# Group outputs scaled behind the next dense part, V copies on two engines, x of chunk 1 behind two Q stores

## The chip, the cores and the metric

The kernel runs on one core of one Trainium2 chip. The metric is the device time of one execution in microseconds; medians of several executions are given, with the lowest and highest beside them. TensorE is called PE, VectorE DVE, ScalarE ACT and GpSimd POOL, as in the profile. The span of a profile is about 2 us shorter than the time of the same execution. "Granted clock" is the share of full speed that the throttle granted TensorE; it is 0.998 to 1.000 unless told otherwise.

## The reference

A transformer block with both branches on the same normalised input, 2048 tokens of 640 features, in bf16:

```python
xn = layernorm(x)                                   # no weights
q, k, v = split(xn @ wqkv)                          # 32 heads of 20
s = q @ k.T * 20 ** -0.5                            # masked: 0 <= i - j < 256
A = (softmax(s) @ v) @ wo
B = (sigmoid(xn @ w_gate) * (xn @ w_up)) @ w_down   # 1536 wide
out = x + A + B
```

## The kernel before

The tokens are worked off in four chunks of 512. Attention runs as a chain of steps (scores, exponentials, masks, product with V), and between two steps a "fill" puts dense matmuls: gate and up, Q, K, V of the next chunk, the down product with Wo. So PE's order is fixed in the program, and PE waits where another engine or a transfer is late. Three PSUM banks (the buffers that PE writes products into; at 51 us PE is listed as waiting 0.34 us for h to free one) turn among all dense products; there is one score buffer, one accumulator `acc`, one `th` tile and five staging tiles `st`.

The loads at the start, all on one issuing queue:

```python
load_gu(0)                   # first half of gate and up weights
load_x(1)                    # x of chunk 1
clear("q", 0); clear("k", 0) # zero the padding of the Q and K scratch
...                          # Q and K of chunk 0, then load_rest()
```

Q and K pass through scratch in device memory; Q is copied by DVE, K by ACT, and both use the `st` tiles, so that the first K copy waits for the first Q store (6.37 us listed in the profile before):

```python
def proj_block(w, c, m):
    ps = ps_d.tile([P, CW], FP32, name="pqk", tag="d")
    ...                                    # 5 matmuls
    st = stp.tile([P, CW], BF16, name="st")
    if w == "q":
        nc.vector.tensor_copy(out=st, in_=ps)
    else:
        nc.scalar.copy(out=st, in_=ps)
    nc.sync.dma_start(out=dst[:, 4 * m:4 * m + 4, :], in_=st)
```

The normalisation of the next chunk runs beside gate and up; POOL computes the reciprocal root:

```python
def rstd_block(mv):
    rstd = lnp.tile([P, 1], FP32, name="rstd")
    nc.gpsimd.tensor_scalar(out=rstd, in0=mv[:, 1:2], scalar1=EPS, scalar2=None, op0=ADD)
    nc.gpsimd.tensor_tensor(out=rstd, in0=rstd, in1=neghalf, op=POW)
    return rstd
```

Gate and up: `th` by ACT from one bank, `h` by DVE from the next. And the end of a head group: DVE transposes the accumulator, then scales it:

```python
def finish_group(c, g, acc):
    t1 = np_.tile([P, 16, 32], FP32, name="t1")
    nc.vector.transpose(out=t1..., in_=acc)
    rec = np_.tile([P, 16, 1], FP32, name="rec")
    nc.vector.reciprocal(rec, t1[:, :, DH:VW])
    for m, slot, first, n in pieces_of(g):
        ...
        nc.vector.tensor_tensor(out=on[m]..., in0=t1..., in1=rec..., op=MULT)
        if slot + n == 32:
            nc.vector.transpose(out=oc[c, m], in_=on[m]...)
```

The fill's order, with the three parts that bring the output weights (`wo_i` is a rearranged copy of Wo in device memory, made by four transfers; `wo` loads it):

```python
fill.add("gu0", ...); fill.add("x2", ...)
fill.add("wd", later(load_wd), 0)
fill.add("qk1", g_qk(1), 50 * MM); fill.add("v1", g_v(1), 40 * 136)
fill.add("wo_i", later(turn_wo), 0)
fill.add("gu1a", ...)
fill.add("wo", later(load_wo), 0)
fill.add("out0", ...)
...
```

The softmax here doesn't subtract the row's maximum and nothing guards it: scores larger than these inputs give would overflow.

Of the kernel before, what the change touches and what calls it, by code (L numbers as in the profile page):

```python
# [18 lines left out]
NCH = S // CW  # L19
SBC = CW // P  # L20
HG = 4
NG = H // HG
# [78 lines left out]
def pieces_of(g):  # L101

    f, left, src = g * DH, DH, 0
    while left:
        m, p = divmod(f, 32)
        n = min(left, 32 - p)
        yield m, p, src, n
        f, left, src = f + n, left - n, src + n
# [3 lines left out]
def kernel(  # L112
# [11 lines left out]
    nc = tc.nc  # L124
# [31 lines left out]
    def load_x(c):  # L156
        t = xp.tile([P, SBC, D], BF16, name="xc")
        xc[c] = t
        nc.sync.dma_start(out=t, in_=xr[:, c * SBC:(c + 1) * SBC, :])
# [33 lines left out]
    def clear(w, k):  # L193
        rows = scratch[w, k].rearrange("(h j) s -> h (j s)", j=32)[:, DH * CW:]
        nc.sync.dma_start(out=rows.rearrange("h (a e) -> h a e", a=4), in_=zero[:, 0:3, :])

    def load_gu(k):
        for t, w in ((wg, B_w_gate), (wu, B_w_up)):
            nc.sync.dma_start(out=t[k], in_=w.rearrange("(c p) f -> p c f", p=P)[:, :, k * FS:(k + 1) * FS])

    load_gu(0)
    load_x(1)
    clear("q", 0)
    clear("k", 0)

# [84 lines left out]
    def proj_block(w, c, m):  # L290


        base = 0 if w == "q" else D
        ps = ps_d.tile([P, CW], FP32, name="pqk", tag="d")
        for d in range(DC):
            wt = wqkv[:, d, base:base + D].rearrange("p (k m) -> p m k", m=DC)
            nc.tensor.matmul(ps, lhsT=wt[:, m, :], rhs=xnT[c][:, d, :],  # L297
                             start=(d == 0), stop=(d == DC - 1))
# [5 lines that stand above are left out]
        dst = scratch[w, c % 2].rearrange("(h j) s -> h j s", j=32)  # L304
        nc.sync.dma_start(out=dst[:, 4 * m:4 * m + 4, :], in_=st)

    def spread(w, c, g0, g1):

        if g0 == 0:
            qk[w, c] = (qp if w == "q" else kp).tile([P, NG, CW], BF16, name=w + "T")  # L310
        src = scratch[w, c % 2].rearrange("(g p) s -> p g s", p=P)
        nc.sync.dma_start(out=qk[w, c][:, g0:g1, :], in_=src[:, g0:g1, :])

    def new_v(c, s):
        v = vp.tile([P, H * VW + 11], BF16, name="v")
        vt[c * SBC + s] = v
        nc.gpsimd.memset(v[:, 0:H * VW].rearrange("p (h d) -> p h d", d=VW)[:, :, DH:VW], 0.5)
        nc.gpsimd.memset(v[:, H * VW:], 0.0)

    def project_v(c, s, hf):  # L320
        ps = ps_d.tile([P, CW], FP32, name="pv", tag="d")
        for d in range(DC):
            nc.tensor.matmul(ps[:, 0:HALF], lhsT=xnT[c][:, d, s * P:(s + 1) * P],  # L323
                             rhs=wqkv[:, d, 2 * D + hf * HALF:2 * D + (hf + 1) * HALF],
                             start=(d == 0), stop=(d == DC - 1))
        return ps

    def copy_v(c, s, hf, ps, copy):
        v3 = vt[c * SBC + s][:, 0:H * VW].rearrange("p (h d) -> p h d", d=VW)
        copy(out=v3[:, hf * 16:(hf + 1) * 16, 0:DH],  # L330
             in_=ps[:, 0:HALF].rearrange("p (h d) -> p h d", d=DH))

    def proj_v(c, s, hf, copy=nc.vector.tensor_copy):
        copy_v(c, s, hf, project_v(c, s, hf), copy)
# [26 lines left out]
    def g_qk(c):  # L361
        for w in "qk":
            for m in range(DC):
                proj_block(w, c, m)
                if w == "k" and m == 1:
                    spread("q", c, 0, NG if c else 2)
                yield 5 * MM
        if c == 0:
            spread("k", c, 0, 1)
            spread("k", c, 1, 3)  # L370
            spread("q", c, 2, 4)
            spread("k", c, 3, 4)

    def g_v(c):
        for s in range(SBC):
            new_v(c, s)
            for hf in range(2):
                proj_v(c, s, hf)
            if s == 0:
                spread("k", c, 0, 2)  # L380
                spread("k", c, 2, NG)
            yield 10 * 136
# [106 lines left out]
    def pv(c, g, parts):  # L489
        acc = ps_a.tile([P, CW], FP32, name="acc")  # L490
        flat = [(pt, *piece[1:]) for step, pt in parts for piece in step["pv"] if piece[0] == g]
        for k, (pt, r, q, n, col) in enumerate(flat):
            v = vt[c * SBC + r]
            for i in range(HG):
                h = g * HG + i
                nc.tensor.matmul(  # L496
                    acc[32 * i:32 * i + 32, q * U:(q + n) * U],
                    lhsT=v[:, h * VW:h * VW + 32], rhs=pt[:, i, col * U:(col + n) * U],
                    start=(k == 0), stop=(k == len(flat) - 1), skip_group_check=True)
        finish_group(c, g, acc)  # L500
# [3 lines left out]
    def finish_group(c, g, acc):  # L504
        t1 = np_.tile([P, 16, 32], FP32, name="t1")
        nc.vector.transpose(out=t1.rearrange("p b r -> p (b r)"), in_=acc)  # L506
        rec = np_.tile([P, 16, 1], FP32, name="rec")
        nc.vector.reciprocal(rec, t1[:, :, DH:VW])
        for m, slot, first, n in pieces_of(g):
            if slot == 0:  # L510
                on[m] = onp.tile([P, 16, 32], BF16, name="on")
            nc.vector.tensor_tensor(out=on[m][:, :, slot:slot + n], in0=t1[:, :, first:first + n],  # L512
                                    in1=rec.to_broadcast([P, 16, n]), op=MULT)
            if slot + n == 32:
                oc[c, m] = op.tile([P, CW], BF16, name="oc")
                nc.vector.transpose(out=oc[c, m], in_=on[m].rearrange("p b r -> p (b r)"))


    class Fill:
        def __init__(self):  # L520
            self.parts = []
            self.done = set()
            self.shut = set()

# [8 lines left out]
        def one(self):  # L533
            label, gen, _ = self.parts[0]
            try:
                cost = next(gen)
                self.parts[0][2] -= cost
                return cost
            except StopIteration:
                self.parts.pop(0)  # L540
                self.done.add(label)
                return 0

        def pull(self, ns):
            while ns > 0 and self.parts and self.parts[0][0] not in self.shut:
                ns -= self.one()
            return ns
# [72 lines left out]
    for _ in g_qk(0):  # L620
        pass
    load_rest()

    fill = Fill()
# [8 lines left out]
    fill.add("x2", later(load_x, 2), 0)  # L633
    fill.add("wd", later(load_wd), 0)
    fill.add("qk1", g_qk(1), 50 * MM)
    fill.add("v1", g_v(1), 40 * 136)
    fill.add("wo_i", later(turn_wo), 0)
    fill.add("gu1a", mix(g_gu(1, 0, 2), norms2, 0, 2, False), 2 * GU)
    fill.add("wo", later(load_wo), 0)
    fill.add("out0", mix(g_out(0), norms2, 0, 2), OUT)  # L640
    fill.add("x3", later(load_x, 3), 0)
    fill.add("qk2", g_qk(2), 50 * MM)
    fill.add("v2", g_v(2), 40 * 136)
    fill.add("gu1b", mix(g_gu(1, 2, 12), g_norms(3, False), 10), 10 * GU)
    fill.add("out1", mix(g_out(1), g_turns(3), 1, 3), OUT)
    fill.add("qk3", g_qk(3), 50 * MM)
    fill.add("v3", g_v(3), 40 * 136)
    fill.add("gu2", g_gu(2, 0, 12), 12 * GU)
    fill.add("out2", g_out(2), OUT)
# [14 lines left out]
    for t, (c, k, step) in enumerate(todo):  # L664
        if k == 0 and c > 0:
            fill.until(f"qk{c}")
        if k == 2 and c > 0:
            fill.until(f"v{c}")
        for group in [x for x in ends if ends[x] == t - 2]:
            pv(*group, parts.pop(group))  # L670
            if group[1] == NG - 1:
                fill.shut.discard(f"out{group[0]}")
        made = (step, scores(c, step))
        for g in dict.fromkeys(piece[0] for piece in step["pv"]):
            parts.setdefault((c, g), []).append(made)
        last, label = next(x for x in cuts if t < x[0])
        credit += fill.left(label) * step["units"] / sum(x[2]["units"] for x in todo[t:last])
        credit = fill.pull(credit)
    fill.pull(10 ** 9)

    c = NCH - 1

# [44 lines left out]
```

## Time and profile before

| | before |
|---|---|
| time, median of 3 runs | 319.24 us (319.14 to 319.47) |
| span of the profile | 317.7 us |
| PE idle in the span | 7.9 us, of which 3.2 are the listed idle time of the five stalls below |

PE is 97% busy, so the table that matters is that of its stalls (listed idle time plus overlap in the list). A stall is told here as the listed idle time plus the time by which matmuls that do not wait overlap in the list. The prediction takes 0.16 us for it. The lines themselves stand in the prediction.

| at us | PE waits for | stall |
|---|---|---|
| 22.4 | a bank that a K copy (ACT) frees, which waits for a Q store | 0.51 |
| 51.1 | a bank that h (DVE) frees | 0.50 |
| 89.1 | Wo | 1.58 |
| 199.5 | a bank that a V copy (DVE) frees | 0.67 |
| 272.3 | the score buffer, behind th and h | 0.66 |

### The profile page before, as it was taken

To read this page: it belongs to the slowest core of one execution; us is meant where nothing else is said; L and a number is where in the kernel's file an instruction comes from. 1 tells how busy PE (TensorE), PEld (TensorE's weight loads), DVE (VectorE), ACT (ScalarE), POOL (GpSimd) and SP (SyncE) were. 2 spreads that over 40 slices of the span, in tenths; PEclk is the share of its full clock that TensorE was granted. 3 is DMA by queue.
4 is the path that set the end of the run, shared out by engine and by line. 5 is a ranking of instruction groups with operands and counts; after the bars stand their busy time and mean duration, and the time that the engine had idled before them with its cause. 6 is when DMAs were issued, how large, how long until landed. Compare 5 with 4: busy or idle time off the path is not lost.

```text
span 317.7 us, 10276 instructions
## 1 busy us (share of the span) xinstructions
PE 309.8 (97%) x4393; PEld 174.6 (55%) x4393; DVE 160.1 (50%) x324; ACT 192.9 (61%) x243; POOL 177.8 (56%) x417
## 2 busy tenths in 40 slices
PE   7999999999989999999999999999999999999996
PEld 3654444456556655544566655544456664444674
DVE  4531486746854564556753553544552544363224
ACT  5713786786845458577654557576765667778200
POOL 3000487667768557575966637476466767576300
PEclk9999999999999999999999999999999999999999
DMA  7976967927744255500045035500000010000002
GB/s 250 371 284 185 321 212 116 314 86 223 233 107 48 64 172 177 182 11 3 0 53 77 23 105 165 186 1 3 2 2 23 26 43 3 2 2 2 0 2 83
DMA packets 34428, 33.05 MB, mean 104 GB/s; under 512 B 9648, under 2 KB 33840, under 8 KB 34352
## 3 DMA queue, kind: packets, MB, share of 16 engines
q1 hardware_dynamic: 34096, 32.17, 34.2%
q8 instruction: 34, 0.56, 0.7%
q10 hardware_dynamic: 288, 0.25, 0.3%
q14 instruction: 10, 0.08, 0.1%
HBM read 21.00 MB, written 10.26 MB: 98 GB/s over the span
## 4 chain that ended last, share of the span: by engine, by line
PE 80%; DMA 7%; ACT 4%; DVE 4%; POOL 2%; issue 1%; SPq 1%; ACTq 0%; POOLq 0%
PE pg L395 14%; PE y L415 14%; PE pu L402 14%; PE pqk L297 10%; PE ps L465 7%; PE acc L496 6%; PE y L428 6%; PE pv L323 5%; DMA wo_i<-in_A_wo_dram 2%; ACT pT L471 2%; DMA sq<-st 2%; PE d L415 2%; DMA sk<-st 1%; POOL pT L475 1%; DMA wo<-wo_i 1%
## 5 line engine op out<-in xcount | busy, mean ns | idle before, releaser
L475 POOL TENSOR_SCALAR_AFFINE_SELECT pT<-pT 128x256 bf16<-128x256 bf16 (+1 forms) x352 | 163.0, 497 | 117.9 <-ACT pT L471 117.8
L471 ACT ACTIVATE pT<-ps 128x1280 bf16<-128x1280 f32 (+2 forms) x152 | 147.4, 1023 | 70.4 <-PE ps L465 64.0
L406 DVE SCALAR_TENSOR_TENSOR h<-th,pu 128x512 bf16<-128x512 f32 x48 | 32.8, 684 | 57.8 <-PE pu L402 32.3
L395 PE MATMUL pg<-xnT,wg 128*128 128x512 bf16 x240 | 59.8, 380 | 0.3 <-DVE h L406 0.3
L402 PE MATMUL pu<-xnT,wu 128*128 128x512 bf16 x240 | 59.8, 380 | 0.0
L415 PE MATMUL y<-wd,h 128*128 128x320 bf16 x336 | 49.4, 300 | 0.0
L297 PE MATMUL pqk<-xnT,wqkv 128*128 128x512 bf16 x200 | 46.2, 381 | 0.4 <-ACT st L303 0.4
L415 PEld LDWEIGHTS <-h 128*128 128x128 bf16 x384 | 36.1, 98 | 14.4 <-issue 0.2
L506 DVE STREAM_TRANSPOSE t<-acc 128x512 f32<-128x512 f32 x32 | 22.8, 712 | 33.3 <-PE acc L496 32.9
L398 ACT ACTIVATE th<-pg 128x512 f32<-128x512 f32 x48 | 28.9, 602 | 17.3 <-DVE h L406 10.0
L402 PEld LDWEIGHTS <-wu 128*128 128x128 bf16 x240 | 22.0, 98 | 25.4 <-issue 0.6
L395 PEld LDWEIGHTS <-wg 128*128 128x128 bf16 x240 | 22.0, 98 | 25.2 <-issue 0.8
L465 PE MATMUL ps<-qT,kT 20*64 20x64 bf16 (+3 forms) x2048 | 32.8, 232 | 0.6 <-ACT pT L471 0.6
L465 PEld LDWEIGHTS <-kT 20*64 20x64 bf16 x2048 | 22.2, 104 | 20.2 <-issue 16.8
L297 PEld LDWEIGHTS <-wqkv 128*128 128x128 bf16 x200 | 22.5, 119 | 18.4 <-issue 1.2
L433 DVE SCALAR_TENSOR_TENSOR xn<-y,xc 128x320 bf16<-128x320 f32 x28 | 13.5, 490 | 30.8 <-PE y L428 30.8
L496 PE MATMUL acc<-pT,v 128*32 128x128 bf16 (+2 forms) x928 | 25.7, 250 | 0.0
L496 PEld LDWEIGHTS <-v 128*32 128x32 bf16 x928 | 16.9, 97 | 15.3 <-issue 11.0
L323 PE MATMUL pv<-wqkv,xnT 128*128 128x320 bf16 x160 | 24.0, 300 | 0.5 <-DVE v L330 0.5
L428 PE MATMUL y<-wo,oc 128*128 128x320 bf16 x140 | 21.2, 299 | 1.4 <-DMA wo<-wo_i 1.4
L512 DVE TENSOR_TENSOR on<-t,rec 128x320 bf16<-128x320 f32 (+4 forms) x48 | 20.5, 428 | 1.1
L428 PEld LDWEIGHTS <-oc 128*128 128x128 bf16 x160 | 15.3, 98 | 7.7 <-issue 1.7
(49 smaller groups left out, 151.3 us busy)
## 6 DMA issues: line engine op xcount, KB each, us to landing
qT<-sq SPq DMA_DIRECT2D x3, 1024.0 KB, 5.9
sq<-st SPq DMA_DIRECT2D x20, 128.0 KB, 2.4
sk<-st SPq DMA_DIRECT2D x20, 128.0 KB, 3.2
out_dram<-xn SPq DMA_DIRECT2D x15, 160.0 KB, 1.8
kT<-sk SPq DMA_DIRECT2D x3, 768.0 KB, 5.6
wg<-in_B_w_gate_dram SPq DMA_DIRECT2D x2, 960.0 KB, 7.6
wu<-in_B_w_up_dram SPq DMA_DIRECT2D x2, 960.0 KB, 12.0
xc<-in_A_x_dram SPq DMA_DIRECT2D x3, 640.0 KB, 12.0
```

Source lines behind the costliest of these rows:

```text
L297: nc.tensor.matmul(ps, lhsT=wt[:, m, :], rhs=xnT[c][:, d, :], start=(d == 0), stop=(d == DC - 1))
L323: nc.tensor.matmul(ps[:, 0:HALF], lhsT=xnT[c][:, d, s * P:(s + 1) * P], rhs=wqkv[:, d, 2 * D + hf * HALF:2 * D + (hf + 1) * HALF], start=( ...
L395: nc.tensor.matmul(pg, lhsT=part(wg, d, f), rhs=xnT[c][:, d, :], start=(d == 0), stop=(d == DC - 1))
L398: nc.scalar.activation(out=th, in_=pg, func=TANH, scale=0.5)
L402: nc.tensor.matmul(pu, lhsT=part(wu, d, f), rhs=xnT[c][:, d, :], start=(d == 0), stop=(d == DC - 1))
L406: nc.vector.scalar_tensor_tensor(out=h, in0=th, scalar=1.0, in1=pu, op0=ADD, op1=MULT)
L415: nc.tensor.matmul(ys[hf], lhsT=ht[c, f][:, s * P:(s + 1) * P], rhs=wd[:, f, hf * HALF:(hf + 1) * HALF], start=(f == 0), stop=False)
L428: nc.tensor.matmul(ys[hf], lhsT=oc[c, m][:, s * P:(s + 1) * P], rhs=wo[:, m, hf * HALF:(hf + 1) * HALF], start=False, stop=(m == DC - 1))
L465: nc.tensor.matmul(ps[hf * U:(hf + 1) * U, i, col * U:(col + n) * U], lhsT=qk["k", kc][32 * i:32 * i + DH, g, key:key + U], rhs=qk["q", c] ...
L471: nc.scalar.activation(out=pt[:, :, to * U:(to + n) * U], in_=ps[:, :, col * U:(col + n) * U], func=EXP, scale=SCALE)
L475: nc.gpsimd.affine_select(out=out, in_=in_, pattern=[[0, HG], [sign, pattern]], compare_op=GE, fill=0.0, base=base, channel_multiplier=-sign)
L496: nc.tensor.matmul(acc[32 * i:32 * i + 32, q * U:(q + n) * U], lhsT=v[:, h * VW:h * VW + 32], rhs=pt[:, i, col * U:(col + n) * U], start=( ...
```

## The change

Its intent: take DVE's work that nobody waits for (the scaling) from ahead of work for which PE waits (h, V and Q copies), split the V copies over two engines, and let the first Q stores go ahead of a load that is needed much later. Its description also names Wo behind the down weights, which holds for both kernels; no line of the diff moves it.

```diff
     load_gu(0)
-    load_x(1)
...
                 proj_block(w, c, m)
+                if c == 0 and w == "q" and m == 1:
+                    load_x(1)
...
-                proj_v(c, s, hf)
+                proj_v(c, s, hf, nc.scalar.copy if hf else nc.vector.tensor_copy)
...
         nc.vector.transpose(out=t1.rearrange("p b r -> p (b r)"), in_=acc)
+        if c < NCH - 1 or g < NG - 1:
+            fill.behind.append(lambda: scale_group(c, g, t1))
+        else:
+            scale_group(c, g, t1)
+
+    def scale_group(c, g, t1):
         rec = np_.tile([P, 16, 1], FP32, name="rec")
...
                 cost = next(gen)
+                if cost:
+                    self.flush()
...
+        def flush(self):
+            while self.behind:
+                self.behind.pop(0)()
...
+            fill.flush()
             pv(*group, parts.pop(group))
...
     fill.pull(10 ** 9)
+    fill.flush()
```

More of the change, by code (lines that the diff above doesn't have):

```diff
@@ L521, in __init__ @@
             self.parts = []
+            self.behind = []
             self.done = set()
```

## The prediction

> **What bounds the kernel now.** I read the page's engine line first, then the list of waits, then the timeline around each wait of TensorE, then how the change reorders each engine's instructions.
>
> ```profile
> span 317.7 us, 10276 instructions
> PE 309.8 (97%) x4393; PEld 174.6 (55%) x4393; DVE 160.1 (50%) x324; ACT 192.9 (61%) x243; POOL 177.8 (56%) x417
> ```
>
> PE is idle for 317.7 - 309.8 = 7.9 us. Summing four-microsecond windows, 1.6 us of that lie in the first 8 us (loads) and 3.1 us behind the last matmul (final add and store). The rest, 3.2 us, is five single waits, and the list of waits has all of them (columns: total us, times, longest):
>
> ```profile
> ACT st L303 <- DMA sq<-st: 6.4, 1, 6.4
> ...
> PE y L428 <- DMA wo<-wo_i: 1.4, 1, 1.4
> ...
> PE ps L465 <- ACT pT L471: 0.6, 1, 0.6
> ...
> PE pv L323 <- DVE v L330: 0.5, 1, 0.5
> ...
> PE pqk L297 <- ACT st L303: 0.4, 1, 0.4
> ...
> PE pg L395 <- DVE h L406: 0.3, 1, 0.3
> ```
>
> A listed matmul's end runs 0.16 us past the point at which the next one could have started (groups of five 512-column matmuls are listed as 1.24 us, but follow each other every 1.08 us). So each stall costs its listed idle time plus 0.16: pqk 0.35 + 0.16 = 0.51 at 22.4 us; pg 0.34 + 0.16 = 0.50 at 51.1; y 1.42 + 0.16 = 1.58 at 89.1; pv 0.51 + 0.16 = 0.67 at 199.5; ps 0.59 + 0.16 = 0.75 at 272.3. Together 4.0 us, 1.26% of 319.24. The order of PE's instructions is the same in both kernels (only which engine some of them wait for differs), so 4.0 us is the most that this change can win in the body.
>
> The three stalls with DVE in them, from the timeline. First the one at 51 us:
>
> ```profile
> 48.03 0.70 DVE L506 STREAM_TRANSPOSE t<-acc 128x512 f32<-128x512 f32 x1
> ...
> 49.93 0.58 POOL L264 TENSOR_TENSOR rstd<-rstd,neghalf 128x1 f32<-128x1 f32 x1
> ...
> 50.60 0.54 DVE L269 TENSOR_SCALAR xn<-xc,mv,rstd 128x640 bf16<-128x640 bf16 x1
> 51.06 0.67 DVE L406 SCALAR_TENSOR_TENSOR h<-th,pu 128x512 bf16<-128x512 f32 x1
> ...
> 51.78 1.24 PE L395 MATMUL pg<-xnT,wg 128*128 128x512 bf16 x5 [0.34 <-DVE h L406]
> ```
>
> PE waits for a PSUM bank that h frees. h stands on DVE behind the scaling of a group (48.77 to 50.6, not shown) and behind xn, whose rstd GpSimd ends at 49.93 + 0.58 = 50.51. Then the one at 199.5 us:
>
> ```profile
> 197.37 0.72 DVE L506 STREAM_TRANSPOSE t<-acc 128x512 f32<-128x512 f32 x1 [0.29 <-PE acc L496]
> ...
> 199.80 1.90 DVE L330 CAST v<-pv 128x320 bf16<-128x320 f32 x4
> ...
> 200.34 0.84 PE L323 MATMUL pv<-wqkv,xnT 128*128 128x320 bf16 x5 [0.51 <-DVE v L330]
> ```
>
> Four V copies pile up behind one group's scaling. And the one at 272 us:
>
> ```profile
> 267.47 0.72 DVE L506 STREAM_TRANSPOSE t<-acc 128x512 f32<-128x512 f32 x1 [1.11 <-PE acc L496]
> ...
> 270.01 0.68 DVE L406 SCALAR_TENSOR_TENSOR h<-th,pu 128x512 bf16<-128x512 f32 x1
> ...
> 270.78 0.60 ACT L398 ACTIVATE th<-pg 128x512 f32<-128x512 f32 x1 [0.91 <-DVE h L406]
> 271.27 1.94 ACT L471 ACTIVATE pT<-ps 128x1024 bf16<-128x1024 f32 x2
> ...
> 273.26 0.43 PE L465 MATMUL ps<-qT,kT 20*64 20x320 bf16 x28 [0.59 <-ACT pT L471]
> ```
>
> Scaling delays h, h holds the single th buffer, th delays the exponentials, and those hold the single score buffer.
>
> [...]at 48.77 DVE does the scaling though h's inputs come ready by 49[...]. [...]The trace has 0.49 us on DVE and 0.43 us for the start's ScalarE copies[...]. [...]the first Q store, issued at 15.94, lands at 22.35 behind loads issued up to ten microseconds before.
>
> **The change part by part.**
>
> (a) x of chunk 1 behind two Q stores. Its 640 KB land at 18.98, wu ahead of it at 17.20, so it takes 1.78 us of the queues. Without it ahead, Q stores 0 and 1 land at 22.35 - 1.78 = 20.57 and 22.66 - 1.78 = 20.88. The first K copy on ScalarE, which waits 6.4 us for the first of these, starts at about 20.7 instead of 22.45 and ends at 21.3. PE wants that bank at 22.58, so the stall of 0.51 us vanishes. Stores 2 to 4 still have the same bytes ahead of them: store 2 lands at 22.98 as before, and the third K copy, which needs its buffer, ends by 23.7, ahead of its bank's next user at 24.7. x itself now lands near 22.7 and is first read at 37.8. Gain 0.51 us.
>
> (b) Scaling behind the next dense part. It deletes nothing: reciprocal 0.25, one or two products (0.2 to 0.7), a transposition of 0.71 when a block fills, some 1.8 us a group, move behind one h, V or Q copy.
> At 51 us: the new order on DVE is t, xn, h, scaling. But xn must wait for the rstd at 50.51, so it starts at 50.55 instead of 50.60, and h at about 51.0 instead of 51.06. The idle DVE time before xn grows by what scaling frees. Gain 0.05 of 0.50 us. The scaling then runs from 51.6 to 53.5; the next h, before at 52.45, waits until then and ends at 54.2, ahead of its bank's next user at 55.0: no new stall.
> At 272 us: the order becomes t, h, scaling. pu starts at 267.72, lasts 1.08 us, and DVE starts 0.25 us later, so h runs from 269.0 to 269.7, not from 270.01. th is then bounded by pg (268.81 plus 1.28, as between pg at 265.40 and th at 266.68): 270.09 instead of 270.78. The exponentials move from 271.27 to 270.58 and end at 272.52; PE could start at 272.51. The stall falls from 0.75 to about 0.06. Gain 0.69 us.
>
> (c) V copies over both engines. For chunks 1 to 3, 12 of 24 move to ScalarE: DVE loses 12 x 0.49 = 5.9 us, ScalarE gains 12 x 0.43 = 5.2, up to 192.9 + 5.2 = 198.1 us. With (b), at 199 us DVE has only t and one V copy ahead of the scaling: PE's block at 199.66 finds its bank free. After that ScalarE's copies wait for the exponentials up to 199.83 and free a bank at 200.4, needed at 200.7; the scaling ends near 200.8 and the next DVE copy at 201.3, needed at 201.4. Both margins are thin, so I count 0.60 of 0.67 us. In chunks 1 and 2 (72 to 80 and 124 to 131 us) ScalarE has gaps of 1.2 to 1.9 and 0.5 to 1.3 us before the exponentials, and PE's three banks rotate slower than a copy of half a microsecond: nothing gained or lost.
>
> (d) Wo behind the down weights: no line of the diff moves it, and on the DMA-issuing queue it stands behind the down weights and chunk 1's K loads in both kernels. The wait of 1.58 us at 89 us is a chain of ScalarE K copies, K stores landing at 77.1, Wo rearranged to 87.7, Wo loaded at 90.7. It starts from PE at 67 us, so it moves with PE, and the stall keeps its length. Gain 0.
>
> Sum: 0.51 + 0.05 + 0.69 + 0.60 = 1.85 us, so 319.24 - 1.85 = 317.4 us.
>
> **The rivals.** First, everything goes, with Wo too: 319.24 - 4.0 = 315.2. Against it: nothing in the diff shortens the Wo chain, and GpSimd is filled from 40.7 to 52.6 us. Second, Wo does not move with PE: its chain has a fixed start and swallows the 0.56 us won before it; 317.95. For it: 5.9 us of it are a 1 MB Q load ahead of K stores. Against it: K copies follow PE's blocks within a microsecond at 66 us. Third, ScalarE becomes the bound by copies ahead of exponentials: each delayed exponential could stall PE by up to 0.5 us, three or four times, for 318.5 to 319.2. Against it: the gaps named in (c); for it, ScalarE is fully busy from 68 to 72 and 192 to 196 us. Fourth, DVE wins both at 51 and elsewhere: 316.9, if the rstd comes earlier than I read.
>
> **Range and chances.** First half 0 to 1.0 us won, second half 0.7 to 1.4, plus 0.2 of scatter between runs (319.14 to 319.47): 316.6 to 318.4, centred on 317.4. Over 2% faster would be under 312.9, more than all idle time of the body, so 1%; slower by 2% needs 6 us of new stalls: 1%. Within 2%: 98%.
>
> **What would show it right or wrong.** Right: PE near 309.8 us busy in a span near 315.9; the waits of pqk on ScalarE and pv on DVE gone, ps on ScalarE gone or under 0.15 us; pg on DVE still about 0.3 us, now with DVE idle before xn; Wo's wait still 1.3 to 1.5 us. Wrong: a wait on Wo over 1.8 us (second rival), PE waiting for v copies of ScalarE or for exponentials near 76, 128 or 201 us (third), or no stall left at 51 us (fourth).

The 0.25 us in (b) from the end of pu to h was its reading; where h waits for pu in the trace before (at 265.68, 271.70 and 274.99 us), it is 0.28 to 0.29 us. In (a), that the Q stores land earlier by just the 1.78 us that x takes is its estimate from the landings at 17.20 and 18.98 us. In (c), PE's blocks of five for V follow each other every 0.70 us in the trace before (1.41 us for two at 195.13), and a V copy takes 0.43 to 0.49; that a delayed exponential could stall PE by up to 0.5 us, in the third rival, is its estimate and was not shown.

## The result, and the profile after

The changed kernel took 317.96 us, median of 4 runs (317.35 to 318.66), against 319.19 (319.09 to 319.47, 4 runs): a ratio of 0.9961, 95% interval 0.9939 to 0.9983. So it is within 2% as predicted, and in the predicted range, 0.6 us above its centre. Ratios are the mean time of one kernel's fast runs over that of the other's of the same rounds, so not quite the ratio of the medians.

The page of the changed kernel, engine line:

```profile
span 316.7 us, 10237 instructions
PE 306.3 (97%) x4353; PEld 174.3 (55%) x4393; DVE 154.4 (49%) x312; ACT 197.9 (63%) x255; POOL 179.4 (57%) x417
```

Twelve V copies have moved: DVE lost 160.1 - 154.4 = 5.7 us (5.9 predicted), ACT gained 5.0 (5.2 predicted). PE's busy time can't be compared: 4393 - 4353 = 40 matmul records are missing from this trace. So I compared when each block of matmuls starts in the two traces, which missing records do not disturb.

The list of waits of the changed kernel (total us, times, longest), cut to the waits for other engines and transfers that bear on PE:

```profile
ACT xn L589 <- DMA xc<-in_A_x_dram: 3.6, 2, 3.0
...
ACT st L302 <- DMA sq<-st: 1.2, 1, 1.2
PE y L429 <- DMA wo<-wo_i: 1.2, 1, 1.2
PE pv L322 <- ACT xnT L277: 1.2, 1, 1.2
```

The four waits of PE for pqk, pg, pv on DVE and ps are gone. The first K copy, at 22.03 us, no longer waits for a Q store: the timeline has its 4.53 us of idle time ended by PE. The wait of 1.2 us for a store that is left is that of the third K copy, at 24.92 us, and PE does not notice it. Wo's wait is there. And there is a new one, of pv on an xnT copy of ACT, with ACT itself waiting 3.0 us for x: at the very start. Before, the timeline had:

```profile
7.48 0.74 ACT L575 ACTIVATE xn<-xc 128x640 bf16<-128x640 bf16 x1 [1.62 <-DMA xc<-in_A_x_dram]
...
13.94 1.24 PE L297 MATMUL pqk<-xnT,wqkv 128*128 128x512 bf16 x5
```

and the changed kernel has:

```profile
8.90 0.74 ACT L589 ACTIVATE xn<-xc 128x640 bf16<-128x640 bf16 x1 [3.01 <-DMA xc<-in_A_x_dram]
...
10.36 0.85 PE L322 MATMUL pv<-wqkv,xnT 128*128 128x320 bf16 x5 [1.17 <-ACT xnT L277]
```

The last rows of x of chunk 0 came 8.90 - 7.48 = 1.42 us later, though no line of the diff touches them: the first Q matmul starts at 15.36 instead of 13.94. This run gave back 1.42 us before the change could win anything. Then, at 51 us:

```profile
50.23 0.22 POOL L262 TENSOR_SCALAR rstd<-mv 128x1 f32<-128x1 f32 x1
50.53 0.58 POOL L263 TENSOR_TENSOR rstd<-rstd,neghalf 128x1 f32<-128x1 f32 x1
...
51.15 0.52 DVE L268 TENSOR_SCALAR xn<-xc,mv,rstd 128x640 bf16<-128x640 bf16 x1 [1.72 <-POOL rstd L263]
51.59 0.67 DVE L407 SCALAR_TENSOR_TENSOR h<-th,pu 128x512 bf16<-128x512 f32 x1
...
52.18 0.24 DVE L515 RECIPROCAL rec<-t 128x16 f32<-128x16 f32 x1
52.31 1.24 PE L396 MATMUL pg<-xnT,wg 128*128 128x512 bf16 x5
```

DVE is idle for 1.72 us before xn, as predicted, and the scaling (rec) comes behind h. But PE's matmul carries no wait: only 0.12 us of the stall of 0.50 are left. At 200 us:

```profile
198.81 0.49 DVE L329 CAST v<-pv 128x320 bf16<-128x320 f32 x1 [0.42 <-PE pv L322]
199.22 0.24 DVE L515 RECIPROCAL rec<-t 128x16 f32<-128x16 f32 x1
...
200.02 0.43 ACT L329 CAST v<-pv 128x320 bf16<-128x320 f32 x1
...
201.11 1.53 PE L322 MATMUL pv<-wqkv,xnT 128*128 128x320 bf16 x10
```

One V copy stands ahead of the scaling, one of ACT beside it, and PE does not wait. At 272 us:

```profile
268.72 0.69 DVE L407 SCALAR_TENSOR_TENSOR h<-th,pu 128x512 bf16<-128x512 f32 x1 [0.89 <-PE pu L403]
269.33 0.25 DVE L515 RECIPROCAL rec<-t 128x16 f32<-128x16 f32 x1
...
269.73 0.60 ACT L399 ACTIVATE th<-pg 128x512 f32<-128x512 f32 x1 [0.22 <-PE pg L396]
270.22 1.93 ACT L472 ACTIVATE pT<-ps 128x1024 bf16<-128x1024 f32 x2
```

h ahead of rec; th now waits for pg and not for h, as the prediction had it, and the exponentials follow at once.

The account of this trace, by the starts of PE's blocks: +1.42 at the start, -0.51 at 22 us, -0.38 at 51, -0.21 at Wo, -0.67 at 200, -0.66 at 272; together -1.01 us, which is the difference of the spans (316.7 - 317.7). The change won 2.22 us without Wo, more than the predicted 1.85, and a late start, which may or may not belong to it, took 1.42 of them. Three questions follow: whose is the late start, which part wins what, and why is the stall at 51 us gone.

### The profile page after: what moved, and what is told of

The parts are those of the page before. It is cut to its first block, busy times and chain, and to the rows that moved or that the text cites. A ratio compares the mean times of both kernels' runs of the same rounds, so it can differ in the third digit from the quotient of the medians.

```text
span 316.7 us, 10237 instructions
## 1 busy us (share of the span) xinstructions
PE 306.3 (97%) x4353; PEld 174.3 (55%) x4393; DVE 154.4 (49%) x312; ACT 197.9 (63%) x255; POOL 179.4 (57%) x417
## 4 chain that ended last, share of the span: by engine, by line
PE 87%; DMA 6%; ACT 2%; issue 2%; SPq 2%; DVE 0%; ACTq 0%
PE pg L396 16%; PE pu L403 16%; PE y L416 14%; PE pqk L296 13%; PE ps L466 8%; PE acc L497 7%; PE y L429 6%; PE pv L322 5%; DMA wo_i<-in_A_wo_dram 2%; DMA xc<-in_A_x_dram 2%; PE d L416 2%; DMA sk<-st 1%; ACT pT L472 1%; DMA wo<-wo_i 1%; SPq L220 1%
## 5 line engine op out<-in xcount | busy, mean ns | idle before, releaser
L476 POOL TENSOR_SCALAR_AFFINE_SELECT pT<-pT 128x256 bf16<-128x256 bf16 (+1 forms) x352 | 165.4, 504 | 115.3 <-ACT pT L472 115.1
L396 PE MATMUL pg<-xnT,wg 128*128 128x512 bf16 x222 | 58.7, 380 | 0.9
L403 PE MATMUL pu<-xnT,wu 128*128 128x512 bf16 x228 | 58.0, 380 | 1.1 <-issue 0.6
L296 PE MATMUL pqk<-xnT,wqkv 128*128 128x512 bf16 x190 | 45.5, 381 | 0.5
L300 DVE CAST st<-pqk 128x512 bf16<-128x512 f32 x20 | 13.7, 690 | 12.2 <-PE pqk L296 11.4
```

What stands on the lines that cost most here:

```text
L296: nc.tensor.matmul(ps, lhsT=wt[:, m, :], rhs=xnT[c][:, d, :], start=(d == 0), stop=(d == DC - 1))
L396: nc.tensor.matmul(pg, lhsT=part(wg, d, f), rhs=xnT[c][:, d, :], start=(d == 0), stop=(d == DC - 1))
L403: nc.tensor.matmul(pu, lhsT=part(wu, d, f), rhs=xnT[c][:, d, :], start=(d == 0), stop=(d == DC - 1))
L476: nc.gpsimd.affine_select(out=out, in_=in_, pattern=[[0, HG], [sign, pattern]], compare_op=GE, fill=0.0, base=base, channel_multiplier=-sign)
```

## The experiments

Twelve experiments ran, each beside the kernel before; two of them repeat a kernel. The three with single groups deferred ran once; all others 4 or 6 times.

| kernel | median us (lowest to highest) | before | ratio (95%) |
|---|---|---|---|
| x moved alone | 319.3 (318.58 to 319.69) | 319.59 | 0.9971 (0.9937 to 1.0005) |
| scaling deferred alone | 318.03 (317.96 to 318.31) | 319.59 | 0.9939 (0.9909 to 0.9969) |
| V copies alone | 319.1 (319.03 to 319.91) | 319.59 | 0.9977 (0.9946 to 1.0008) |
| changed kernel again | 317.43 (317.08 to 320.03) | 319.59 | 0.993 (0.9893 to 0.9968) |
| scaling and copies, x in place | 317.38 (317.3 to 318.78) | 319.33 | 0.9946 (0.992 to 0.9973) |
| wo_i right behind wd | 317.54 (317.21 to 318.13) | 319.33 | 0.9943 (0.9922 to 0.9964) |
| wo_i among the Q blocks | 317.39 (317.07 to 317.73) | 319.33 | 0.9936 (0.9917 to 0.9956) |
| wo_i early | 316.21 (315.79 to 317.36) | 319.33 | 0.9895 (0.9873 to 0.9917) |
| first group deferred | 319.37, once | 319.59 | |
| second group deferred | 319.64, once | 319.59 | |
| both deferred | 320.22, once | 319.59 | |
| wo_i early again | 316.39 (315.93 to 318.45) | 319.59 | 0.991 (0.9882 to 0.9939) |

The kernel before scattered from 319.19 to 322.55 in the first lot (its slowest run at a clock of 0.995), from 318.95 to 320.29 in the second, from 319.04 to 320.51 in the third. So single times say little within 1 us.

### Each part alone, and the whole again

x alone keeps only the moved load; scaling alone keeps only the deferral; copies alone keeps only this line:

```diff
-                proj_v(c, s, hf)
+                proj_v(c, s, hf, nc.scalar.copy if hf else nc.vector.tensor_copy)
```

> Only x of chunk 1 is moved behind two Q stores. If the stalls of TensorE simply add up, only the stall of 0.51 us at 22 us goes and the other four keep their lengths (0.50, 1.58, 0.67, 0.75): 0.5 us faster than before, ratio 0.9984. Rival, that the move is what made the start of the changed kernel late by 1.4 us: the first Q or K matmul starts later than 14.5 us here too, and the time is the same as before or longer.

> Only the scaling is deferred. My theory now: the stall at 51 us falls from 0.50 to about 0.15 us, because the products of the scaling no longer hold up GpSimd's small rstd instructions (each of them about 0.22 us, where before two of them took 0.46 and 0.31); the stall at 272 us goes from 0.75 to under 0.15; the one at 200 us only shrinks, from 0.67 to 0.4 to 0.6, since all V copies still queue on VectorE behind the scaling one part later; 22 us keeps 0.51, 89 us keeps 1.4 to 1.6. Sum 1.1 to 1.3 us faster, ratio 0.9962. Rival, as predicted: the stall at 51 us keeps 0.45 us because rstd comes no earlier, ratio 0.9972.

> Only the V copies are halved. The first DVE copy still stands behind a whole scaling until 199.8 us and frees the bank that the stalled block waits for, so the stall at 200 us keeps 0.6 to 0.7 us and the others keep theirs: ratio 1.000, within 0.1 us. Rival: fewer copies on VectorE are what removes it, stall gone and 0.7 us faster, ratio 0.998.

> The changed kernel once more, for the scatter of its start. If the late start of its first profile (first Q matmul at 15.4 us, not 13.9) was chance, most of these runs are near 317.3 us, 1.9 us (0.6%) faster than before, with single runs up to 1.4 us longer, and the profile shows the first Q matmul near 14 us and stalls of 0 to 0.15 at 22, 51, 200 and 272 us, 1.3 to 1.6 at 89. If the change causes the late start, the mean stays near 318.0 and the profile has it again.

What each trace's PE blocks show against the kernel before, in us (negative is won):

| | predicted | changed | x alone | scaling alone | copies alone | scaling and copies |
|---|---|---|---|---|---|---|
| start of the first Q block | 0 | +1.42 | +0.21 | +0.30 | +0.25 | +0.07 |
| stall at 22 us | -0.51 | -0.51 | -0.51 | -0.50 | -0.31 | -0.33 |
| stall at 51 us | -0.05 | -0.38 | +0.02 | -0.39 | +0.01 | -0.41 |
| wait for Wo | 0 | -0.21 | +0.31 | -0.01 | -0.55 | -0.35 |
| stall at 200 us | -0.60 | -0.67 | 0 | -0.33 | 0 | -0.67 |
| stall at 272 us | -0.69 | -0.66 | 0 | -0.66 | 0 | -0.66 |

Each column sums to the difference of the spans within 0.1 us.

**The stall at 200 us needs two parts.** With the copies alone, four DVE copies became two, but the scaling still stood ahead of them, and PE waited as long as before (0.51 listed). With the deferral alone, the stall moved to 201.2 us and shrank to 0.34. Only both together end it. **The stalls at 51 and 272 us belong to the deferral alone.** The copies alone won nothing that their trace shows, apart from a shorter wait for Wo and a shorter stall at 22 us, neither of which they can reach; both turn out below to vary by themselves. Their interval includes 1, and so does that of x alone.

Run again, the changed kernel had a median of 317.43. Its profiled run fell on a clock of 0.995 and took 320.03; its trace shows PE behind by 1.67 us near 92 us, where ten output matmuls took 2.58 us (1.52 in the trace before), and has the same gains of 0.51, 0.38, 0.67 and 0.66 elsewhere. The start was late again, by 0.64.

Several expectations missed: the stall at 22 us with the deferral alone (0.01) and with the copies alone (0.20, both expected 0.51), the stall at 200 us with the deferral alone (0.34, expected 0.4 to 0.6), the wait for Wo in three kernels (1.89, 1.03 and 1.88 us for x alone, copies alone and the whole again; expected 1.58, 1.58 and 1.3 to 1.6), and the start of the changed kernel run again (14.58, expected near 14).

The x move does its work as predicted. In the trace of x alone:

```profile
17.80 0.58 SPq L159 DMA_DIRECT2D xc<-in_A_x_dram  x1
...
20.83 0.59 ACT L302 CAST st<-pqk 128x512 bf16<-128x512 f32 x1 [4.53 <-PE pqk L296]
```

x is issued behind two Q stores; the first K copy starts at 20.83 instead of 22.45 (20.7 predicted), and what releases it is PE, no longer the store. But the deferral alone has no stall at 22 us either, with x in its old place. That needed the next run.

### Without the x move

```diff
     load_gu(0)
+    load_x(1)
...
-                if c == 0 and w == "q" and m == 1:
-                    load_x(1)
```

> The change without its first part: scaling deferred and V copies halved, x of chunk 1 where it was. If the two together remove the stall at 200 us that neither removes alone (0.34 us of it left with the scaling alone, 0.67 with the copies alone), VectorE's v wait is gone here; the stalls at 51 and 272 us are gone as with the scaling alone; those at 22 us (0.2 to 0.5) and 89 us (1.0 to 1.9) stay. Against before 1.6 to 1.9 us faster, ratio 0.9945; against the whole change 0.3 to 0.5 us slower.

It came to 317.38 us, 1.95 below the kernel before, with a stall of 0.18 us at 22 us. The whole change, run again, had 317.43, which was 2.16 below its own. It was run at another time. So the 0.3 to 0.5 us that this kernel was expected to lose against the whole change do not show; 0.2 us can't be told from the scatter. In its list of waits one wait of PE for anything outside it is left:

```profile
PE y L428 <- DMA wo<-wo_i: 1.1, 1, 1.1
```

So what is the x move worth? All profiles taken, in us:

| profile | x moved | first Q block | first K copy | stall at 22 | Wo needed at | wait for Wo |
|---|---|---|---|---|---|---|
| before | no | 13.94 | 22.45 | 0.51 | 89.23 | 1.58 |
| copies alone | no | 14.19 | 22.39 | 0.20 | 89.19 | 1.03 |
| scaling alone | no | 14.24 | 22.24 | 0.01 | 88.63 | 1.57 |
| scaling and copies | no | 14.01 | 22.19 | 0.18 | 88.56 | 1.23 |
| first deferred | no | 14.19 | 22.26 | 0.07 | 88.81 | 1.71 |
| second deferred | no | 14.06 | 22.89 | 0.82 | 89.48 | 1.28 |
| both deferred | no | 15.08 | 22.39 | 0.00 | 89.51 | 1.84 |
| x alone | yes | 14.15 | 20.83 | 0.00 | 88.95 | 1.89 |
| changed | yes | 15.36 | 22.03 | 0.00 | 89.75 | 1.37 |
| changed again | yes | 14.58 | 21.26 | 0.00 | 88.97 | 1.88 |
| wo_i right behind wd | yes | 14.26 | 20.93 | 0.00 | | 0.14 |
| wo_i among Q | yes | 14.17 | 20.85 | 0.00 | | 0 |
| wo_i early | yes | 15.48 | 22.30 | 0.00 | | 0 |
| wo_i early again | yes | 14.79 | 21.47 | 0.00 | | 0 |

With x in its old place, the first K copy starts between 22.19 and 22.89, though PE's first Q block starts between 13.94 and 15.08: the load queue sets it (in the trace before, ACT is idle 6.37 us ahead of this copy, until the Q store lands). The stall is then 0 to 0.82 us, 0.26 on average over seven profiles; the 0.51 of the kernel before was one draw. The largest is in the trace with the second group deferred. ACT and PE there:

```profile
22.89 1.56 ACT L303 CAST st<-pqk 128x512 bf16<-128x512 f32 x3 [6.68 <-PE pqk L297]
...
23.52 1.67 PE L297 MATMUL pqk<-xnT,wqkv 128*128 128x512 bf16 x7 [0.66 <-ACT st L303]
```

(The release of the copy is put down to PE there; in the trace before, it is the Q store's. It must be the store here too: six of the seven profiles with x moved name PE as well, and start this copy 6.67 to 6.68 us behind the first Q block, which would be 20.73. The seventh, `wo_i` early, names the store and has 6.82.) With x moved, the stall is always nil, and the first K copy follows the first Q block by 6.67 to 6.82 us in all seven profiles. So the move saves just the stall. Where the start is late there is none to save: in the old order PE would have waited at 22 us anyway, and the late start takes the place of that wait (15.08 with no stall at all).

Late starts of a microsecond or more appear in 3 of 14 profiles: twice with x moved, once (15.08) with it in its old place. The move takes a load out of the early queue and adds none ahead of the rows in question, and the old order shows a late start too. So I take it for chance; with three cases that is argued and not shown, and what makes the rows late is open.

### Wo earlier

The wait for Wo is the largest stall left. Over the ten profiles with `wo_i` in its old place it is 1.03 to 1.89 us, 1.54 on average. If it had a fixed end, as the second rival says, it would shrink by 1 us for every us that PE comes later; a line fitted through the ten rows gives -0.09 us per us, with a standard error of 0.27. So it moves with PE on average, as the prediction has it, with a scatter that I had not allowed for.

Three kernels, all made from the changed one, issue the four transfers of `wo_i` earlier. First right behind the down weights, ahead of the Q and K of chunk 1, which is what the description of the change says literally:

```diff
     fill.add("wd", later(load_wd), 0)
+    fill.add("wo_i", later(turn_wo), 0)
     fill.add("qk1", g_qk(1), 50 * MM)
     fill.add("v1", g_v(1), 40 * 136)
-    fill.add("wo_i", later(turn_wo), 0)
```

> The changed kernel with what its title says of Wo done in fact: the rearrangement of Wo is issued right behind the down weights, ahead of chunk 1's Q and K stores. If the wait for Wo at 89 us is only a matter of its late issue, it is gone and the time falls by 1.2 to 1.9 us against the changed kernel, to about 315.9 us. Rival: its 0.8 MB, in four transfers of 5 to 7 us, now hold up the Q stores that follow in the same queue, the first K copy waits for its staging buffer beyond 66 us, and TensorE stalls at 66 to 75 us by up to 3 us, which gives back part or all.

The second takes `wo_i` out of the fill and issues it between the last two Q blocks of chunk 1 (in the trace before, the DMA share is 0.37 from 64 to 68 us and 0.27 from 68 to 72; it is not the least of the trace, 0.04 from 96 to 100):

```diff
                 proj_block(w, c, m)
+                if c == 1 and w == "q" and m == 4:
+                    turn_wo()
```

> The changed kernel with the rearrangement of Wo issued behind chunk 1's last Q store, at about 66 us, where the queues are least busy. If queue order decides, the wait at 89 us is gone, no Q store is held up, and the K stores and loads come 1 to 3 us later: kT of chunk 1 lands near 83 to 85 us, with the first scores of chunk 1 at 85. Expected 315.9 us, with 0 to 1 us lost if kT is late.

The third issues it at the end of `load_rest`, that is before gate and up of chunk 0 (its old place in the fill is taken out here too):

```diff
         clear("k", 1)
+        turn_wo()
```

> The changed kernel with the rearrangement of Wo issued at the end of the early loads, near 38 us. The wait at 89 us is gone. The transposes of x of chunk 1, the down weights and the Q stores come up to 5 us later in the queue; the first K copy of chunk 1 may wait for the first Q store, with a stall of 0 to 3 us near 66 us. If that slack suffices 315.9 us, else 316 to 319.

The first two took the wait for Wo away (0.14 and 0 us left) and won nothing: 317.54 and 317.39 us, beside 317.38 for scaling and copies. The transfers stand ahead of something else in the queue. Behind the down weights they delay the Q stores; a K copy waits 2.3 us for its `st` tile, the exponentials behind it on ACT come late, and PE waits for the score buffer. PE's timeline of that kernel:

```profile
69.81 0.42 PE L466 MATMUL ps<-qT,kT 20*64 20x320 bf16 x16 [1.30 <-ACT pT L472]
```

Among the Q blocks they delay the K of chunk 1, which comes back from scratch at 82.7 us:

```profile
82.77 0.43 PE L468 MATMUL ps<-qT,kT 20*64 20x320 bf16 x28 [1.51 <-DMA kT<-sk]
```

So the wait of 1.5 us had been turned into one of 1.30 + 0.07 and one of 1.51 + 0.07 us. Issued early, at about 38 us, when no store is urgent, the transfers delay nothing that PE notices. PE's timeline in the repetition of that kernel:

```profile
88.33 0.99 PE L417 MATMUL y<-wd,h 128*128 128x320 bf16 x6
89.16 1.52 PE L430 MATMUL y<-wo,oc 128*128 128x320 bf16 x10
```

The output product follows the down product with no wait. The times are 316.21 and 316.39 us. This is the fastest version here: about 1.2 us below scaling and copies, and 3.1 and 3.2 us below the kernel before, which is 1% and thus still within 2%. Its ratios to the kernel before, 0.9895 and 0.991, have intervals below 1. Its repetition started at 14.79 us, a little outside what was expected; the rest came as expected.

> The best kernel so far again, for its size: 316.0 to 316.4 us median, ratio to before 0.989 to 0.991, no wait for Wo and no new stall of TensorE over 0.2 us between 25 and 300 us. Its profile had a late start (first Q matmul at 15.5 us); if that is chance and not the kernel's, it is at 13.9 to 14.6 here.

### Why the stall at 51 us went

The prediction let h come 0.05 us earlier, since xn must wait for its rstd. In the traces the rstd itself comes earlier. POOL's work is the same in both kernels, so I looked at the length of its instructions. In the kernel before, DVE and POOL together:

```profile
42.52 0.51 DVE L512 TENSOR_TENSOR on<-t,rec 128x320 bf16<-128x320 f32 x1
42.66 0.46 POOL L263 TENSOR_SCALAR rstd<-mv 128x1 f32<-128x1 f32 x1
...
49.05 0.71 DVE L512 TENSOR_TENSOR on<-t,rec 128x192 bf16<-128x192 f32 x1
...
49.53 0.31 POOL L263 TENSOR_SCALAR rstd<-mv 128x1 f32<-128x1 f32 x1
```

These two rstd instructions, the first and fourth of the chunk, lie over a product of the scaling and take 0.46 and 0.31 us; the second and third, which do not, take 0.22 and 0.22. The first ends at 43.12 just behind the product (43.03), the fourth at 49.84 just behind the other (49.76). It is so beyond this chunk: over all three chunks that this trace normalises in this way, POOL's first rstd instruction takes 0.21 to 0.22 us in the six cases without a product over it, and 0.31 to 0.48 in the six in which a product is already running.

The theory: the deferral moves two products off two rstds. The first group's product sits on the first rstd (0.46), the second group's on the fourth (0.31). To tell this from a pure change of DVE's order, deferral was limited to one group, the other, or both, of chunk 0, with everything else as in the kernel before:

```diff
-        if c < NCH - 1 or g < NG - 1:
+        if (c, g) in ((0, 0),):          # or ((0, 1),) or ((0, 0), (0, 1))
             fill.behind.append(lambda: scale_group(c, g, t1))
```

> The kernel before, with the scaling deferred for the first group of chunk 0 alone (the one at 42 us). [...]GpSimd's first rstd instruction takes 0.22 to 0.24 us, not 0.46, and the fourth rstd is ready some 0.2 us earlier, but VectorE is then still in the second group's scaling until the old time, so h starts where it did (19.25 us after the first scores) and the stall keeps 0.45 to 0.50 us (listed 0.3 to 0.35). Rival, that the wait for GpSimd alone sets h: the stall shrinks by 0.2.

> The kernel before, with the scaling deferred for the second group of chunk 0 alone (the one at 48 us, directly ahead of the stalled h). [...]the fourth rstd instruction takes 0.22 us, not 0.31, the first keeps 0.46; rstd is ready 0.1 us earlier than before, h starts 0.1 to 0.2 us earlier (19.05 to 19.15 after the first scores), the stall falls to 0.30 to 0.40. Rival, that it is only the order of h and scaling: all 0.38 us are won here. Rival as I predicted: 0.05.

> Scaling deferred for these two groups alone. If the two parts are all there is to the stall at 51 us, h starts 18.85 to 18.9 us after the first scores and the stall falls to 0.10 to 0.15 us, as where every group is deferred; the stalls at 200 and 272 us keep 0.67 and 0.75, since their groups are not deferred.

| | first rstd instruction, ns, blocks 1 to 4 | 4th rstd done, us from first scores | h starts | stall at 51 us |
|---|---|---|---|---|
| before | 457, 219, 215, 313 | 18.69 | 19.25 | 0.50 |
| first group deferred | 227, 222, 215, 314 | 18.46 | 19.02 | 0.27 |
| second group deferred | 457, 221, 216, 217 | 18.59 | 19.07 | 0.32 |
| both deferred | 231, 223, 220, 218 | 18.39 | 18.87 | 0.12 |
| all deferred (scaling alone) | 228, 224, 218, 218 | 18.39 | 18.86 | 0.12 |

Each deferral shortens just the rstd instruction under its own product, and the two gains of 0.23 and 0.18 us together are near the 0.38 of both. Deferring the first group was expected to leave the stall as it was, and that was a miss; the rival named there, 0.2 us, came true. The first rstd is 8 us ahead of the stall, but POOL works without a gap from 40.7 to 52.6 us, so what the first rstd saves shifts everything behind it on POOL, the fourth rstd too. DVE moves along: xn of the third block waits for its rstd, the second group's transposition stands behind it and starts 15.99 us after the first scores instead of 16.22, and its scaling, which I had expected to end at the old time, ends 0.23 us earlier too. The second group's 0.18 are 0.10 of rstd and 0.08 of h coming sooner behind it; the latter is near the 0.05 that the prediction had seen. The single times of these three runs (319.37, 319.64, 320.22) show nothing of it: the third had the late start of 15.08.

What makes the instruction longer was not shown: no run here tests a cause. What the runs show is the coincidence, and that the instruction is short again once the product is moved (0.23 and 0.22 us, in the table above). Over all 14 traces, each of the 40 first rstd instructions that start under a running product takes 0.31 to 0.48 us and ends 0.08 to 0.09 us behind the product. But a product is not the only thing that does it. In the kernels with every group deferred, 11 others take 0.28 to 0.29 us with a normalisation (xn) running over them, and end 0.07 to 0.08 us behind that; a twelfth under an xn was not longer. With the scaling alone:

```profile
96.92 0.70 DVE L269 TENSOR_SCALAR xn<-xc,mv,rstd 128x640 bf16<-128x640 bf16 x1
...
97.41 0.29 POOL L263 TENSOR_SCALAR rstd<-mv 128x1 f32<-128x1 f32 x1
```

All the rest take 0.21 to 0.23 us.

## Why the prediction was right or wrong

The time was predicted at 317.4, in 316.6 to 318.4; it was 317.96 in the first result, and 317.43 run again. The class was right. Two errors of size met in the sum, and a scatter came on top.

- **(a), x, 0.51 us: right mechanism, mis-sized term.** The stores land earlier, as worked out, and the stall goes. But 0.51 was the stall of one profile; seven have 0.26 on average, and scaling and copies without the x move could not be told from the whole. Not seen at all: with a late start there is no stall to save. The first profiled run started 1.42 us late, and gained 1.01 us instead of 2.4.
- **(b) at 51 us, 0.05 us: the step that failed.** It reads: "But xn must wait for the rstd at 50.51, so it starts at 50.55 instead of 50.60". That took POOL's end as given. Moving DVE's products off POOL's instructions brought the rstd 0.30 us forward, and the stall lost 0.38. The fourth rival ("if the rstd comes earlier than I read") named the possibility without a cause.
- **(b) at 272 us, 0.69: right.** 0.66 measured, by the predicted chain: th waits for pg. The stall was never 0.75: ahead of scores the term to add is 0.07 us and not 0.16, so the gain is the whole stall, and the most that the change could win in the body is 3.92 us and not 4.0.
- **(c), 0.60: right.** 0.67 measured, and only with (b), as argued; neither part alone does it.
- **(d), 0: right on average.** "The stall keeps its length" is wrong for a single run: it is 1.54 us on average, from 1.03 to 1.89. By the slope above, PE's lead does not shorten or lengthen it. The wait of over 1.8 us, which the prediction names as a sign of its second rival, came in three of ten profiles, the changed kernel run again among them (1.88): with this scatter it does not tell the two apart.
- **The rivals.** The first (all stalls go) fell with the wait for Wo. The second (Wo swallows the early gains) did not happen, by the slope above. The third (ACT's copies stall PE) left no stall in any trace. ACT carries 5.0 us more and PE does not wait for it.
- **What was not foreseen:** starts up to 1.4 us late, in 3 of 14 profiles. The prediction allowed 0.2 us of scatter between runs; the changed kernel's first four runs span 1.3.

With the terms at their measured size, the sum is 0.26 + 0.38 + 0.67 + 0.66 = 1.97 us. The medians have 319.59 - 317.43 = 2.16 for the changed kernel run again; the two can't be told apart within the scatter.

## What to carry to other kernels

When work is moved on one engine, look at what ran beside it on the other engines (here VectorE's products beside GpSimd's small instructions, which took 0.31 to 0.48 us there and 0.21 to 0.22 without): the end of the fourth rstd, read from the old profile, moved by 0.30 us. A stall that hangs on a transfer should be sized from several profiles (the one at 22 us was 0 to 0.82 us in seven), and taking it away can uncover scatter that it had absorbed (in the old order, the start at 15.08 us left no stall). When a transfer is moved ahead in a queue, look at what stands behind it: of three places here, two gave the whole gain back (317.54 and 317.39 us, beside 317.38), and the third won about 1.2 us.
